# A causal dynamic convolution with layer norm and feed-forward net on one core: shorter softmax and norm steps, a first part summed by TensorE in four chunks, low halves of the weights on VectorE, and a new written order

## The chip, the cores and the metric

The kernel runs on one core of a Trainium2 chip. The metric is the device time of one launch in microseconds (us), the median of several runs; lower is better. The engines of the core are named as in the profile: PE is TensorE (matmul) and PEld its loading of weights, DVE is VectorE, ACT is ScalarE, POOL is GpSimd, SP is the engine that only issues transfers (SPq, POOLq and ACTq are the queues of issues).

## The reference

The input `x` has 8 batches of 4224 tokens of 192 features; `weight_gen` gives each token 8 heads of 7 taps. A softmax over the taps weighs a causal convolution, head by head (24 features each); a layer norm and a feed-forward net of width 768 follow, with a residual.

```python
w = weight_gen - np.max(weight_gen, axis=-1, keepdims=True)
w = np.exp(w)
w = w / (np.sum(w, axis=-1, keepdims=True) + 1e-09)
x_pad = np.concatenate([np.zeros((B, 6, D)), x], axis=1)
x_unf = x_pad[:, np.arange(S)[:, None] + np.arange(7)[None, :], :].reshape(B, S, 7, 8, 24)
x = np.einsum('bshk,bskhg->bshg', w, x_unf).reshape(B, S, D)
mu, var = mean and variance of x over its 192 features
xn = (x - mu) / np.sqrt(var + 1e-06) * g_ln
return x + np.maximum(xn @ w_ch1, 0.0) @ w_ch2      # 192 -> 768 -> 192
```

`g_ln`, `w_ch1` and `w_ch2` come as doubles.

## The kernel before

**Layout.** Each of the 128 partitions holds 264 consecutive tokens ("columns"); 16 partitions make a batch. The columns are cut three ways: into parts for the norm (six of 4, six of 8, fifteen of 12, one of 8, one of 4), into pieces for the softmax (4, 8, then 12 each), and into groups of four columns for the feed-forward net, 66 in all. A part is made of chunks of 4 or 6 columns for the convolution.

**Softmax**, piece by piece: maximum on VectorE (`max`), subtraction on GpSimd (`sub`), exponential on ScalarE (`exp`), sum on VectorE (`sum`, into an SBUF tile `sm`), an estimate of the inverse on ScalarE from logarithm and exponential (`rcp`), one Newton step on VectorE in three instructions that work in the PSUM tile `wn` (`inv`), and the product of exponentials and inverse into `wn` (`mul`).

**Convolution**, chunk by chunk. Taps 1 and 2, 3 and 4, 0, and 5 and 6 are multiplied by four instructions, `c0` to `c3`, into pair buffers `pr` (tap 0 into the output buffer `y`). Two transfers that GpSimd issues add one half of a pair to the other (`d0`, `d1`), and four additions on GpSimd sum up (`a0` to `a3`, L514). The first three chunks go another way: TensorE sums the seven products in PSUM by matmuls with an identity matrix (`z0` to `z3`, L532), ScalarE copies the sum out (L539), and the fourth product is GpSimd's, with weights that ScalarE has copied to SBUF (`keep`, L471).

**Norm and transposition.** ScalarE sums and squares each column; per part it takes the inverse root (logarithm, exponential, square: `rstd`), and VectorE refines it in five instructions (`newton`). Per group ScalarE scales (`xh`) and rounds to fp16 (`hi`, L635), GpSimd subtracts for the low half (`lo`, L648), and SP issues a transposing transfer (`turn`, L652) into `xT`. Such a transfer and GpSimd's adding transfers are kept apart by waits.

**Feed-forward net.** A group's first layer is three units of 72 half-row matmuls each, listed as x36 (L670), every unit into one of two PSUM buffers `ph`. ScalarE's relu makes the fp16 high half `hh` (L685), VectorE the low half `hlo` (L687); the `ph` buffer is free only after `hlo`. The second layer is two half outputs per group (`p0`, `p1`, L721) into the one buffer `po`, put in between the next group's units; VectorE merges `po` with the residual in `y` (`f`, L773), and SP stores. The last group's output has a form of its own (L750).

**Weights.** They are loaded as pairs of 32-bit words, turned to fp32 by bit operations on VectorE (L836 to L846), and scaled by powers of two that come from their norm (`w_scale`, L860 to L876). ScalarE makes a scaled fp16 high half and, in a second copy, a scaled fp32; GpSimd subtracts for the low half (`w_l`, L905 for the first layer, L938 for the second). For the first layer SP then swaps row halves by four transfers (`w_m`, L909), `c_w` to `c_w`. Every unit waits for all of these. Before the first unit, 11 matmuls without use for the result run on TensorE (`wake`, L642), as soon as the first high half is there.

**Order.** A table, `PLACE`, gives every operation one number; all are issued in that order, so each engine works off its own list in the order of the numbers and waits at an instruction until what it needs is there. Buffers are assigned in the same order.

## Time and profile before

| | |
|---|---|
| median of 3 runs | 869.25 us (866.22, 869.25, 870.33) |
| span of the profiled execution | 867.2 us (no other time is recorded for it) |
| TensorE busy, share of the span | 823.4 us, 95% |
| VectorE | 772.1 us, 89% |
| ScalarE | 683.7 us, 79% |
| GpSimd | 679.6 us, 78% |
| first feed-forward unit starts | 64.04 us |
| last product ends | 862.9 us |

The profile is of one execution. A busy share is a mean over the whole span: it doesn't say which engine the others wait for at a given time. Matmuls overlap in their pipeline, so rows of several matmuls give from the first start to the last end.

### The profile page before, as it was taken

The numbers are of one execution on the slowest core, as the hardware profiler recorded it, in microseconds if no ns is written. First come the engines' busy times: TensorE is split into PE (matmuls) and PEld (weight loads), VectorE is DVE, ScalarE is ACT, GpSimd is POOL, SyncE is SP. The second block draws the span as 40 slices with busy tenths as digits, with TensorE's granted clock in tenths as the row PEclk, the third lists the DMA queues.
The fourth block names the chain that finished last, engine by engine and source line by source line (L and its number), as shares of the span: only waits on it lengthen the run. The fifth ranks groups of instructions, "written<-read, shape, count | busy, mean of one in ns | idle before, by whom it ended". The sixth has DMA issues, their size and how long they took to land.

```text
span 867.2 us, 37431 instructions
## 1 busy us (share of the span) xinstructions
PE 823.4 (95%) x16665; PEld 787.7 (91%) x16665; DVE 772.1 (89%) x796; ACT 683.7 (79%) x1781; POOL 679.6 (78%) x390
## 2 busy tenths in 40 slices
...
GB/s 193 190 127 166 166 163 184 200 176 180 194 193 151 220 94 188 213 181 180 160 205 195 149 213 175 165 139 187 207 99 200 120 151 190 124 127 106 40 76 110
DMA packets 137465, 140.89 MB, mean 162 GB/s; under 512 B 107479, under 2 KB 109015, under 8 KB 137303
## 3 DMA queue, kind: packets, MB, share of 16 engines
...
q8 instruction: 130, 2.13, 1.1%
q14 instruction: 32, 0.26, 0.1%
q10 hardware_dynamic: 304, 0.00, 0.0%
...
## 4 chain that ended last, share of the span: by engine, by line
PE 68%; DVE 9%; issue 2%; DVEq 0%
PE ph L670 34%; PE po L721 34%; DVE pr L511 4%; DVE hlo L687 2%; DVE y L511 1%; DVE y L773 1%; PE ph L750 1%; DVE sm L449 0%; DVE mx L440 0%; DVE wn L465 0%; DVE wn L460 0%; DVE wn L461 0%; DVE wn L459 0%; DVE wn L599 0%; DVE wn L601 0%
## 5 line engine op out<-in xcount | busy, mean ns | idle before, releaser
L514 POOL TENSOR_TENSOR y<-y,pr 128x1152 f32<-128x1152 f32 (+1 forms) x192 | 474.5, 2499 | 39.0 <-DVE pr L511 22.1
L670 PE MATMUL ph<-xT,c_w 64*128 64x256 f16 x7128 | 420.0, 270 | 10.5 <-DVE hlo L687 7.8
L670 PEld LDWEIGHTS <-c_w 64*128 64x128 f16 x7128 | 377.6, 94 | 28.3 <-issue 13.5
L721 PE MATMUL po<-c_w2h,hh 64*128 64x192 f16 x3120 | 392.5, 243 | 1.4 <-issue 1.0
L721 PE MATMUL po<-c_w2h,hlo 64*128 64x192 f16 x3120 | 392.4, 243 | 0.5 <-issue 0.5
L721 PE MATMUL po<-c_w2l,hh 64*128 64x192 f16 x3120 | 392.4, 243 | 0.0
L721 PEld LDWEIGHTS <-hh 64*128 64x128 f16 x6240 | 345.7, 94 | 2.8 <-issue 1.9
L511 DVE TENSOR_TENSOR pr<-x,wn 128x2304 f32<-128x2304 f32 (+1 forms) x150 | 332.5, 2226 | 6.6 <-POOL y L514 1.8
L687 DVE SCALAR_TENSOR_TENSOR hlo<-ph,hh 128x1024 f16<-128x1024 f32 x198 | 239.2, 1219 | 57.2 <-ACT hh L685 56.9
L685 ACT ACTIVATE hh<-ph 128x1024 f16<-128x1024 f32 x198 | 200.3, 1015 | 105.2 <-PE ph L670 101.7
L721 PEld LDWEIGHTS <-hlo 64*128 64x128 f16 x3120 | 225.5, 94 | 0.7 <-issue 0.7
L648 POOL TENSOR_TENSOR hl<-xh,hl 128x768 f16<-128x768 f32 x66 | 115.0, 1748 | 44.5 <-ACT hl L635 33.0
L615 ACT ACTIVATE xh<-y,s 128x192 f32<-128x192 f32 x264 | 125.5, 535 | 16.1 <-DVE s L603 12.5
L569 ACT ACTIVATE junk<-y,s 128x192 f32<-128x192 f32 x264 | 119.6, 453 | 6.9
L517 POOL DMA_DIRECT2D pr<-pr x96 | 94.4, 1082 | 37.3 <-DMA xT<-hl 14.2
L564 ACT ACTIVATE junk<-y 128x192 f32<-128x192 f32 x264 | 95.1, 360 | 13.6 <-POOL y L514 7.2
L773 DVE SCALAR_TENSOR_TENSOR y<-po,c_fs,y 128x768 f32<-128x768 f32 (+1 forms) x80 | 67.9, 860 | 5.4 <-PE po L721 5.4
L511 DVE TENSOR_TENSOR y<-x,wn 128x1152 f32<-128x1152 f32 (+1 forms) x51 | 60.0, 1181 | 0.1
L635 ACT ACTIVATE hl<-xh 128x768 f16<-128x768 f32 x66 | 55.0, 837 | 2.1 <-DMA xT<-hl 1.1
L564 ACT ACTIVATION_READ_ACCUMULATOR junk<-y 128x1 f32 x264 | 49.5, 188 | 0.0
L569 ACT ACTIVATION_READ_ACCUMULATOR junk<-y,s 128x1 f32 x264 | 49.4, 187 | 0.0
L532 PE MATMUL ph<-pr,ident 128*128 128x384 f32 x72 | 27.1, 531 | 16.5 <-DVE pr L511 15.6
...
## 6 DMA issues: line engine op xcount, KB each, us to landing
...
```

The lines of the kernel that those rows point to most:

```text
L511: E.tensor_tensor(out=ov, in0=xv, in1=wv, op=ALU.mult)
L514: Q.tensor_tensor(out=flat(0), in0=flat(0), in1=flat(k), op=ALU.add)
L517: return Q.dma_start(flat(to), flat(k), accum_op=ALU.add, max_dma_last_dim=CHUNK * D * 4)
L564: A.activation(junk, at(y)[:, j, :], AF.Identity, scale=-1.0 / D, accum_out=at(s4)[:, 3, t : t + 1])
L569: A.activation(junk, at(y)[:, j, :], AF.Square, bias=at(s4)[:, 3, t : t + 1], accum_out=at(s4)[:, 0, t : t + 1])
L615: A.activation(paired(xh, t), at(y)[:, i, :].rearrange("p (c q) -> p c q", q=P // 2), AF.Identity, bias=at(s4)[:, 3, g + t : g + t + 1], s ...
L648: lambda xh=xh, hl=hl: Q.tensor_tensor(out=halves(hl, True), in0=pairs(xh), in1=halves(hl, False), op=ALU.subtract),
L670: T_.matmul(ph[:, r, v * 2 * P : (v + 1) * 2 * P], W["w1"][rows, WB[r][c], w, f : f + P], xv[rows, a, c, :, :], start=(v == 0 and k == 0), ...
L685: lambda: A.activation(at(hh)[:, us, :], at(ph), AF.Relu), [ph], [(hh, u)])
L687: lambda: V.scalar_tensor_tensor(out=at(hlo)[:, us, :], in0=at(ph), scalar=0.0, in1=at(hh)[:, us, :], op0=ALU.max, op1=ALU.subtract),
L721: made.append(T_.matmul(at(po)[:, z, e * D : (e + 1) * D], token(b, 2 * z + e, j)[rows], W[w][rows, j, :], start=(ph == 0 and e == 0 and k ...
L773: V.scalar_tensor_tensor(out=ysl, in0=at(po)[:, zs[0] : zs[-1] + 1, : 2 * D], scalar=W["fs"][:, 0:1], in1=ysl, op0=ALU.mult, op1=ALU.add)
```

## The change

- **Softmax.** The sum goes straight to PSUM, ScalarE reads it there, and the Newton step has two instructions for three. Two places in PSUM take turns.
- **Norm.** The square is written by ScalarE to PSUM with the scale in it, and `newton` has four instructions for five; two places take turns.
- **Start of the convolution.** The first part's four columns come as two chunks of two; the first four chunks (the first 12 columns, as before) are summed by TensorE, and GpSimd multiplies two of the four pairs (taps 3 and 4, and 5 and 6).
- **Weights.** The low halves are made on VectorE in one instruction that scales and subtracts; the scaled fp32 copies are gone. The second layer's scaled copy is gone as well.
- **The first half outputs** stand behind all three units of the second group, where they stood behind its second and third.
- **Order.** `PLACE` is new throughout.

```diff
 PARTS = (4,) * 6 + (8,) * 6 + (12,) * 15 + (8, 4)
-DIRECT = 3
+DIRECT = 4
+BY_POOL = (3, 5)
 PLACE = {
-    'w_l': (153, 156),
+    'w_l': (137, 166),
...
-            m = min(CHUNK, n - o) if n % CHUNK == 0 else min(4, n - o)
+            m = 2 if s0 == 0 else min(CHUNK, n - o) if n % CHUNK == 0 else min(4, n - o)
...
-        ps = WN[:, S0_ : S0_ + m]
+        ps = WN[:, S0_ + turn * MMAX : S0_ + turn * MMAX + m]
 
         step("V", v_ns(m * K), "sum",
-             lambda: V.tensor_reduce(out=at(sm)[:, :m], in_=at(e)[:, :m], axis=AX.X, op=ALU.add), [e], [sm])
+             lambda: V.tensor_reduce(out=ps, in_=at(e)[:, :m], axis=AX.X, op=ALU.add), [e], [sm])
...
-            A.activation(at(rr)[:, :m], at(sm)[:, :m], AF.Ln, bias=bias[:, 1:2])
+            A.activation(at(rr)[:, :m], ps, AF.Ln, bias=bias[:, 1:2])
...
-            V.tensor_scalar(out=ps, in0=at(sm)[:, :m], scalar1=1e-9, scalar2=None, op0=ALU.add)
-            V.tensor_tensor(out=ps, in0=ps, in1=r, op=ALU.mult)
+            V.scalar_tensor_tensor(out=ps, in0=ps, scalar=1e-9, in1=r, op0=ALU.add, op1=ALU.mult)
...
-            if direct and i == 3:
-                op("Pool", q_ns(2 * nd), (f"c{i}", t0), lambda k=k: mul(k, 2, Q), [*xr, (ch["soft"]["e"], "w")], w)
+            if direct and k in BY_POOL:
+                op("Pool", 1.89 * 2 * nd, (f"c{i}", t0), lambda k=k: mul(k, 2, Q), [*xr, (ch["soft"]["e"], "w")], w)
...
-            A.activation(row(2), row(1), AF.Square)
+            A.activation(aux(0), row(1), AF.Square, scale=D**-0.5 / A2)
...
-            V.tensor_scalar(out=aux(0), in0=row(0), scalar1=1.0 / (D * A2 * A2), scalar2=1e-6 / (A2 * A2),
-                            op0=ALU.mult, op1=ALU.add)
-            V.tensor_tensor(out=aux(1), in0=aux(0), in1=row(2), op=ALU.mult)
+            V.scalar_tensor_tensor(out=aux(1), in0=row(0), scalar=1e-6 * D, in1=aux(0), op0=ALU.add, op1=ALU.mult)
...
-        def low(dst, src, hi, n, r, w):
-            op("Pool", q_ns(n), ("w_l", 0), lambda: Q.tensor_tensor(out=dst(), in0=src(), in1=hi(), op=ALU.subtract), r, w)
+        def low(dst, src, hi, n, r, w, scale):
+            op("V", v_ns(n), ("w_l", 0),
+               lambda: V.scalar_tensor_tensor(out=dst(), in0=src(), scalar=scale, in1=hi(), op0=ALU.mult,
+                                              op1=ALU.subtract), r, w)
...
-        copy("w_h", lambda: f32(wa, F), lambda: f32(wa, F), F, ["gi"], [wa], gi[:, 0:1])
-        low(lambda: w1[:, 0, 1, :], lambda: f32(wa, F), lambda: w1[:, 0, 0, :], F, [wa, "h0"], ["l0"])
+        low(lambda: w1[:, 0, 1, :], lambda: f32(wa, F), lambda: w1[:, 0, 0, :], F, [wa, "gi", "h0"], ["l0"], gi[:, 0:1])
...
-        op("Pool", q_ns(NF * D), want2,
-           lambda: Q.tensor_tensor(out=w2g, in0=f32(w2r, NF * D), in1=w2f, op=ALU.subtract),
-           ["w2h", "fs", *wv], ["w2"])
+        op("V", v_ns(NF * D), want2,
+           lambda: V.scalar_tensor_tensor(out=w2g, in0=f32(w2r, NF * D), scalar=r2[:, 2:3], in1=w2f, op0=ALU.mult,
+                                          op1=ALU.subtract),
+           ["w2h", "r2", "fs", *wv], ["w2"])
...
+            late = prev["prev"] is not None and prev["prev"]["prev"] is None
             for u in range(3):
                 products(prev, u)
-                if u and prev["prev"]:
+                if u and prev["prev"] and not late:
                     half_output(prev["prev"], u - 1, prev["s"])
+            if late:
+                for z in range(2):
+                    half_output(prev["prev"], z, prev["s"])
```

The new order, at three places. The names are the buffers with their numbers. First GpSimd's list at the start, from its first product to the first group's low half (`hl0`); before, it read:

```order
L511 TENSOR_TENSOR pr0_76<-x_63,e0_98 128x2x768
L442 TENSOR_TENSOR e0_98<-w2_66,mx0_92 128x672
L511 TENSOR_TENSOR pr2_78<-x_63,e1_99 128x2x768
L511 TENSOR_TENSOR pr4_80<-x_63,e1_99 128x2x768
L442 TENSOR_TENSOR e0_98<-w0_64,mx1_93 128x672
L442 TENSOR_TENSOR e1_99<-w1_65,mx0_92 128x672
L517 DMA pr3_79<-pr3_79 128x768
L648 TENSOR_TENSOR hl0_83<-xh0_81,hl0_83 128x2x384
L514 TENSOR_TENSOR y3_70<-y3_70,pr0_76 128x768
L905 TENSOR_TENSOR c_w1_127<-hlo0_90,c_w1_127 128x768
```

And now (L517 is the product, L449 the softmax's subtraction, L655 the low half; the code above them is longer by some lines):

```order
L517 TENSOR_TENSOR pr3_79<-x_63,e1_97 128x2x384
L517 TENSOR_TENSOR pr0_76<-x_63,e1_97 128x2x384
L449 TENSOR_TENSOR e1_97<-w2_66,mx0_92 128x672
L517 TENSOR_TENSOR pr4_80<-x_63,e0_96 128x2x768
L517 TENSOR_TENSOR pr2_78<-x_63,e0_96 128x2x768
L517 TENSOR_TENSOR pr3_79<-x_63,e0_96 128x2x768
L517 TENSOR_TENSOR pr2_78<-x_63,e0_96 128x2x768
L449 TENSOR_TENSOR e1_97<-w0_64,mx1_93 128x672
L523 DMA pr4_80<-pr4_80 128x768
L449 TENSOR_TENSOR e0_96<-w1_65,mx0_92 128x672
L655 TENSOR_TENSOR hl0_83<-xh0_81,hl0_83 128x2x384
```

Ahead of the low half stand four wide products where two stood (a third, of the first chunk, was earlier), and four of half the width, two of them shown; the weights' low halves (L905) are gone from the list.

Second, SP's list around the first two transpositions. Before (`c_w1` is the first layer's weights; L909 swaps their row halves):

```order
L909 DMA c_w1_127<-c_w1_127 64x1536
L422 DMA w1_65<-in_weight_gen_dram 128x1x672
L909 DMA c_w1_127<-c_w1_127 64x2x384
L909 DMA c_w1_127<-c_w1_127 64x1536
L652 DMA_TRANSPOSE xT0_85<-hl0_83 128x12x128
L909 DMA c_w1_127<-c_w1_127 64x2x384
L652 DMA_TRANSPOSE xT1_86<-hl1_84 128x12x128
```

Now:

```order
L427 DMA w0_64<-in_weight_gen_dram 128x1x672
L659 DMA_TRANSPOSE xT0_85<-hl0_83 128x12x128
L918 DMA c_w1_125<-c_w1_125 64x1536 x2
L427 DMA w1_65<-in_weight_gen_dram 128x1x672
L918 DMA c_w1_125<-c_w1_125 64x2x384 x2
L659 DMA_TRANSPOSE xT1_86<-hl1_84 128x12x128
```

The first transposition stood behind three of the four swaps and now stands ahead of all.

Third, VectorE's list around the first two `hlo`. Before (L511 are products, L687 is `hlo`, L459 to L461 a softmax's Newton step):

```order
L511 TENSOR_TENSOR y6_73<-x_63,wn0_104 128x768
L511 TENSOR_TENSOR y7_74<-x_63,wn0_104 128x768
L511 TENSOR_TENSOR y8_75<-x_63,wn0_104 128x768
L687 SCALAR_TENSOR_TENSOR hlo0_90<-ph1_106,hh0_88 128x1024
L459 TENSOR_SCALAR wn0_104<-sm0_96 128x96
L460 TENSOR_TENSOR wn0_104<-wn0_104,rr0_94 128x96
L461 SCALAR_TENSOR_TENSOR wn0_104<-wn0_104,rr0_94 128x96
L687 SCALAR_TENSOR_TENSOR hlo0_90<-ph0_105,hh0_88 128x1024
```

Now (L517 and L694):

```order
L517 TENSOR_TENSOR pr1_77<-x_63,wn0_102 128x2x768
L517 TENSOR_TENSOR pr3_79<-x_63,wn0_102 128x2x768
L517 TENSOR_TENSOR pr4_80<-x_63,wn0_102 128x2x768
L870 TENSOR_SCALAR c_r2_123<-po0_105 128x1
L466 SCALAR_TENSOR_TENSOR wn0_102<-wn0_102,rr0_94 128x96
L467 SCALAR_TENSOR_TENSOR wn0_102<-wn0_102,rr0_94 128x96
L517 TENSOR_TENSOR pr2_78<-x_63,wn0_102 128x2x768
L694 SCALAR_TENSOR_TENSOR hlo0_90<-ph0_103,hh0_88 128x1024
L471 TENSOR_TENSOR wn0_102<-e1_97,wn0_102 128x672
L880 TENSOR_SCALAR c_r2_123<-c_r2_123 128x1
L882 TENSOR_SCALAR c_r2_123<-c_r2_123 128x1
L883 RECIPROCAL c_r2_123<-c_r2_123 128x1
L694 SCALAR_TENSOR_TENSOR hlo0_90<-ph1_104,hh0_88 128x1024
```

The first `hlo` stood behind three products of one tap and now stands behind four of two taps, the last of them directly ahead of it.

## Rows read from the trace of the kernel before

**Rows 1.** The first part of the page: busy time of each engine, its share of the span, and its instructions.

```profile
PE 823.4 (95%) x16665; PEld 787.7 (91%) x16665; DVE 772.1 (89%) x796; ACT 683.7 (79%) x1781; POOL 679.6 (78%) x390
```

**Rows 2.** The span cut into stretches. The columns are the stretch and its length, the busy time (and instructions) of PE, PEld, DVE, ACT and POOL, the granted share of TensorE's clock, the share in which the DMA engines are busy, and GB/s.

```profile
0.00:20.00 20.00, 6.33 (x11) 3.53 (x12) 12.84 (x25) 4.79 (x12) 7.50 (x11) 1.00 0.77 197
20.00:40.00 20.00, 17.13 (x55) 9.94 (x55) 16.96 (x28) 14.46 (x46) 5.90 (x3) 1.00 0.81 212
...
100.00:200.00 100.00, 100.00 (x2136) 100.00 (x2132) 98.57 (x112) 86.81 (x231) 94.41 (x64) 1.00 0.80 178
...
300.00:400.00 100.00, 99.98 (x2129) 99.53 (x2125) 99.10 (x92) 86.95 (x230) 91.30 (x48) 1.00 0.85 175
...
700.00:800.00 100.00, 100.00 (x2133) 99.49 (x2129) 78.60 (x78) 78.62 (x205) 81.10 (x45) 1.00 0.68 137
```

**Rows 3.** From the chain of work that ended last: start, us, engine, output and line, instructions. The first two are the pairs of units of two neighbouring groups, the third is the last group's output.

```profile
282.87 3.93 PE ph L670 x72
...
294.71 3.93 PE ph L670 x72
...
856.81 6.06 PE ph L750 x72
```

**Rows 4.** TensorE's and VectorE's instructions in order of time where the feed-forward net begins: start, us, engine, line, operation, tiles and shapes, count, and in brackets how long the engine stood idle before and what released it. x72 is two units, x36 one.

```profile
59.45 4.66 PE L642 MATMUL ph<-hl 128*128 128x512 f16 x11
64.04 4.10 PE L670 MATMUL ph<-xT,c_w 64*128 64x256 f16 x72
...
72.08 1.22 DVE L687 SCALAR_TENSOR_TENSOR hlo<-ph,hh 128x1024 f16<-128x1024 f32 x1
...
73.35 6.08 PE L670 MATMUL ph<-xT,c_w 64*128 64x256 f16 x72 [5.21 <-DVE hlo L687]
...
81.60 0.22 PEld L721 LDWEIGHTS <-hh 64*128 64x128 f16 x4
```

**Rows 5.** The same view of VectorE, ScalarE, GpSimd and SP's queue between 10 and 60 us.

```profile
11.77 1.75 DVE L511 TENSOR_TENSOR pr<-x,wn 128x1536 f32<-128x1536 f32 x1 [1.80 <-DMA x<-in_x_dram]
...
25.82 0.80 ACT L539 COPY y<-ph 128x768 f32<-128x768 f32 x1 [5.07 <-PE ph L532]
...
36.06 2.91 POOL L511 TENSOR_TENSOR pr<-x,e 128x1536 f32<-128x1536 f32 x1 [6.03 <-ACT pr L849]
...
42.90 0.83 ACT L635 ACTIVATE hl<-xh 128x768 f16<-128x768 f32 x1
...
44.79 1.94 POOL L648 TENSOR_TENSOR hl<-xh,hl 128x768 f16<-128x768 f32 x1
...
53.09 1.19 POOL L905 TENSOR_TENSOR c_w<-hlo,c_w 128x384 f16<-128x384 f32 x1
...
56.39 1.60 SPq L652 DMA_TRANSPOSE xT<-hl  x1
...
58.05 0.64 SPq L909 DMA_DIRECT2D c_w<-c_w  x1
```

**Rows 6.** Transfers issued in the first 90 us: what, the queue, how many, KB each, median us from issue to landing.

```profile
x<-in_x_dram SPq DMA_DIRECT2D x1, 900.0 KB, 7.8
...
c_w<-c_w SPq DMA_DIRECT2D x2, 96.0 KB, 3.9
```

**Rows 7.** Instructions grouped by line and shape over the whole span, of VectorE and then of GpSimd: line, engine, operation, tiles, shapes, count | busy us, mean ns of one | idle before.

```profile
L511 DVE TENSOR_TENSOR pr<-x,wn 128x2304 f32<-128x2304 f32 x90 | 228.4, 2545 | 0.6 <-POOL y L514 0.3
L511 DVE TENSOR_TENSOR pr<-x,wn 128x1536 f32<-128x1536 f32 x60 | 104.1, 1746 | 6.0 <-DMA x<-in_x_dram 1.8 <-POOL y L514 1.6 <-PE po L860 1.4
...
L511 DVE TENSOR_TENSOR y<-x,wn 128x1152 f32<-128x1152 f32 x30 | 40.4, 1345 | 0.1
...
L459 DVE TENSOR_SCALAR wn<-sm 128x96 f32<-128x96 f32 x21 | 5.3, 254 | 0.2
...
L597 DVE TENSOR_SCALAR wn<-s 128x12 f32<-128x12 f32 x15 | 2.5, 169 | 0.8 <-ACT junk L569 0.2
...
L846 DVE SCALAR_TENSOR_TENSOR hlo<-pr,po 128x384 f32<-128x384 f32 x3 | 1.6, 544 | 0.0
...
L846 DVE SCALAR_TENSOR_TENSOR hlo<-pr,ph 128x768 f32<-128x768 f32 x1 | 0.9, 947 | 0.0
...
L514 POOL TENSOR_TENSOR y<-y,pr 128x768 f32<-128x768 f32 x72 | 143.8, 2045 | 10.6 <-DVE y L511 4.8 <-DVE pr L511 2.5 <-DMA pr<-pr 1.8
...
L511 POOL TENSOR_TENSOR pr<-x,e 128x1536 f32<-128x1536 f32 x3 | 8.7, 2904 | 17.5 <-ACT e L471 7.2 <-ACT pr L849 6.0 <-DMA x<-in_x_dram 4.3
L938 POOL TENSOR_TENSOR c_w2l<-hlo,c_w2h 128x1152 f16<-128x1152 f32 x1 | 3.0, 3002 | 0.0
L905 POOL TENSOR_TENSOR c_w<-hlo,c_w 128x768 f16<-128x768 f32 x1 | 1.6, 1642 | 0.0
```

**Rows 8.** VectorE's and TensorE's instructions in order of time around 174 us, columns as in rows 4: the 27th `hlo`, and the two units beside it.

```profile
173.44 1.22 DVE L687 SCALAR_TENSOR_TENSOR hlo<-ph,hh 128x1024 f16<-128x1024 f32 x1
...
173.66 4.11 PE L670 MATMUL ph<-xT,c_w 64*128 64x256 f16 x72
```

**Rows 9.** What TensorE waited for between 95 and 790 us: us in total, how many times, the longest.

```profile
PE ph L670 <- issue: 2.5, 2, 1.4
PE ph L670 <- DVE hlo L687: 2.3, 5, 1.0
PE po L721 <- issue: 1.5, 2, 1.0
```

More of the change, by code (lines that the diff above doesn't have):

```diff
@@ new lines @@
+    'w_load': (23, 1, 6, 25, 3, 5),
+    'w_load2': (52,),
+    'w_as': (77,),
+    'w_av': (78, 79, 80, 86),
+    'w_an': (91,),
+    'w_cs': (44,),
+    'w_cv': (24, 36, 37, 45),
+    'w_cn': (46,),
+    'w_s1': (111, 115, 122, 127, 132),
+    'w_h': (133, 148),
+    'w_l': (137, 166),
+    'w_m': (149, 147, 170, 172),
+    'w_c2s': (96, 140, 174),
+    'w_c2v': (84, 90, 93, 97, 130, 135, 139, 145, 157, 163, 167, 178),
+    'w_c2n': (100, 150, 179),
+    'w_s2': (189, 196, 205, 213, 215, 217, 228),
@@ new lines @@
+    'max': (12, 8, 43, 63, 101, 171, 218, 424, 314, 496, 694, 584, 939, 1108, 930, 1111, 1263, 1261, 1498,
+        1560, 1644, 1739, 1923),
+    'sub': (14, 10, 57, 114, 124, 229, 334, 435, 564, 666, 773, 874, 959, 1153, 1078, 1257, 1386, 1449,
+        1588, 1690, 1796, 1876, 1967),
+    'exp': (16, 15, 64, 123, 156, 264, 371, 473, 577, 674, 786, 929, 1025, 1173, 1109, 1270, 1448, 1455,
+        1597, 1697, 1817, 1892, 1976),
+    'sum': (21, 17, 67, 126, 160, 325, 388, 485, 601, 718, 812, 947, 1027, 1186, 1137, 1271, 1454, 1485,
+        1602, 1781, 1863, 1990, 1992),
@@ new lines @@
+    'squares': (88, 81, 128, 116, 162, 169, 186, 193, 253, 260, 269, 288, 312, 305, 355, 357, 385, 418, 426,
[7 rows of a table added]
+    'rstd': (89, 129, 175, 206, 268, 301, 358, 430, 505, 576, 649, 735, 822, 919, 1026, 1120, 1234, 1325,
+        1414, 1530, 1617, 1720, 1831, 1929, 2024, 2121, 2226, 2301, 2348),
+    'newton': (95, 134, 180, 223, 279, 322, 364, 443, 511, 590, 655, 748, 825, 921, 1030, 1122, 1237, 1328,
[13 rows of a table added]
+    'wake': (138,),
[4 rows of a table added]
+    'turn': (146, 176, 237, 247, 329, 374, 407, 417, 475, 467, 556, 546, 636, 625, 689, 681, 775, 785, 851,
[21 rows of a table added]
@@ L199 @@
+    'halo': (245, 645, 891, 1138, 1378, 1780, 2076),
+    'unit': (187, 195, 219, 221, 235, 236, 261, 276, 289, 304, 315, 333, 345, 360, 372, 394, 395, 415, 428,
[11 rows of a table added]
+    'relu': (204, 202, 220, 231, 244, 256, 273, 278, 297, 318, 321, 346, 366, 363, 381, 397, 409, 421, 440,
[11 rows of a table added]
+    'hlo': (214, 208, 232, 234, 262, 257, 283, 299, 307, 331, 342, 352, 369, 367, 384, 406, 410, 425, 447,
[15 rows of a table added]
+    'hop': (248, 290, 338, 386, 414, 445, 487, 518, 566, 609, 641, 679, 712, 747, 788, 807, 855, 889, 918,
[17 rows of a table added]
 }
@@ L326 @@
     S0_ = MMAX * K
-    X0_ = S0_ + MMAX
+    X0_ = S0_ + 2 * MMAX
+    assert X0_ + 6 * PMAX <= 2 * HALF
     def at(b):
```

88 lines of the change are left out of this document (28 added, 60 removed), and 240 rows, old and new, of the table PLACE.

## The prediction

> **What bounds the kernel now.** I read the busy shares first, then the slices by stretch, then TensorE's own row of instructions, and last the lists of VectorE and GpSimd around the place where TensorE's stream begins. TensorE is busy 823.4 us of 867.2 [rows 1], and from 100 us on it is busy without a break [rows 2]: a group of four columns takes 294.71 - 282.87 = 11.84 us there [rows 3], and 66 groups are 781.4 us. The last product ends at 856.81 + 6.06 = 862.87 [rows 3]; what follows to 867.2 is 4.3 us of merge and store. The first feed-forward product starts at 64.04 [rows 4]. So the span is 64.0 (start) + 781.4 + 4.3 + 17.4 us in which the stream stood still. Of these 17.4, one stretch lies at the start: by 81.60, where the first half output begins, five units are done [rows 4]; five units are 5 x 1.97 = 9.8 us of the 17.56 since 64.04, so 7.7 is lost. The other 9.7 is scattered over 780 us.
>
> The second thing to see is VectorE: 98.6 us of the 100 from 100 on and 99.1 of the 100 from 300 on, and only 78.6 from 700 to 800 [rows 2]. For the first half of the run it has as little room as TensorE; later it has much. An instruction saved on VectorE late in the run is worth nothing; one saved before the stream starts, or while VectorE is full, may be.
>
> So the time can change in three ways: the stream starts earlier, it stands still for less at the start, or VectorE and GpSimd (94.4 and 91.3 us of 100 in the same stretches) fail to follow a stream that is earlier. TensorE's own work is the same: 198 units, 130 half outputs, the last four outputs; the first part is split, but its columns are gathered either way.
>
> **What is removed and added, on VectorE.** All durations are rows 7. Each softmax loses one step of three: 23 x 0.25 = 5.8 us. Each norm loses one of five: 29 x 0.17 = 4.9 us. The products of taps 3 and 4 of the first 12 columns go to GpSimd: 3 x 1.75 = 5.2 us. Three low halves come from GpSimd: 0.95 + 0.55 + 1.34, 2.8 us if they cost as the other steps of these widths. Net -13 us, of which the 10.7 in small steps is spread over the run; after 400 us VectorE's own idle time hides it. The reductions now write PSUM and ScalarE reads it; the old first step already read one memory and wrote the other at 254 ns, so I put the move at nothing, bounds -0.1 and +0.1 us each; 23 of them make 2 us at most, late ones hidden.
>
> GpSimd gains 3 x 2.90 = 8.7 us of products and loses 1.64 + 1.19 + 3.00 = 5.8 (two rows of low halves, the third estimated from the row at 53.09 [rows 5]). ScalarE loses three copies of the weights, some 2.8 us; it is busy 79% [rows 1] and on the path only where it evicts the first units.
>
> **The start, step by step.** Before, the first unit hangs on two chains [rows 5]. One is part 0: gathered and copied at 25.82, high half at 42.90, low half 44.79 to 46.7, and then the transposition is issued only at 56.39, because on SP it stands behind three of the weights' swaps (the second fence of rows of the order). The third waits for GpSimd's second low half (53.09), and the fourth swap is issued last, at 58.05; its row lands in 3.9 us [rows 6]. The wake-up products from 59.45 end at 64.1.
>
> After, the transposition stands ahead of all swaps on SP, and the low halves stand on VectorE. I walk down the lists with the row durations. The first x load is 720 KB for 900 KB, so the first product starts about 0.8 us before 11.77 [rows 5, 6]. Columns 0 to 3 come as two small chunks; the second is gathered and copied by 24, against 25.82. GpSimd then runs four wide products in a row, 4 x 2.9, with one stop: the third needs a buffer that ScalarE holds for the weights until about 30.5. It ends near 36, where before its third product began (36.06). High half near 37, low half on GpSimd near 40 to 42, transposition near 44. The weights: VectorE's second low half stands 70 instructions into its list, near 50.5 to 51; the swaps are issued at 51 and 51.7 and land 3.9 later: the first unit starts near 55.6, 8.4 earlier.
>
> The eviction that frees the third unit is a second, independent reading. Before, VectorE's list up to and with its first `hlo` has 106 instructions whose rows sum to 68.1 us; it ends at 72.08 + 1.22 = 73.30 [rows 4], 5.2 later (it stands idle for 10.2 us in the first 40 alone [rows 2]; neighbours overlap a little). After, that list has 87 instructions and 57.4 us: 7.8 less of products, 2.7 of softmax steps, 1.4 of norm steps, 1.5 more of weights. With 5.2 again it ends at 62.6; ScalarE's list, which must evict first, reaches that point near 63.3 in the walk, so I take 63.9. The third unit then starts at 64.0 for 73.35. The fourth `hlo` stands 8.8 us of rows later, at 72.7; the sixth unit starts at 73.5 and the first half output at 75.4. Taking off the sixth unit, which the new order puts ahead of it, this is 73.5 against 81.60: the stream is 8.1 ahead.
>
> Two charges. The first two units run after a pause of some 8 us behind the wake-up products; before, a pause of 5.2 us was followed by units at the lower clock (6.08 for 3.93 [rows 4]). That costs up to 1.9 per unit, but both wait for the eviction at 63.3 anyway: nothing, at most 1.9. And the low halves read both operands from SBUF on VectorE while GpSimd adds; no row of before shows such a pair. Bounds: nothing, and one add of 2.05 [rows 7] for each of the two ahead of the first unit, 4.1. I take 1. The stream is 7.1 ahead.
>
> **Does it stay ahead?** VectorE is full, so `hlo` can't come earlier than its list lets it. Before, the 27th `hlo` ends at 174.66, and the unit that needs its buffer starts at 175.6, 1.0 later [rows 8]. After, the list up to the 27th `hlo` is 168.0 for 173.1: 5.1 shorter. So about there the stream can be 5.1 + 1.0 = 6.1 ahead, no more. The other places are looser (8 us shorter at the 50th, 8.4 at the 100th, 12.7 at the end). Past the tight place TensorE is the bound again, and part of the 2.3 us that it waited for `hlo` between 95 and 790 [rows 9] goes, some 1. The 4.0 of "issue" waits stays. Gain: 6.1 + 1 = 7.1, less 0.5 for GpSimd, whose list before the low half of the 22nd group is 4.6 longer. 6.6 off 867.2 is 860.6, and 862.5 as a median if the profiled span stands to the runs as before (867.2 to 869.25).
>
> **Rivals.**
> - *The lead is given back (866.5).* If GpSimd's four products and the buffer that ScalarE holds push parts 3 to 5 back, VectorE and GpSimd are both full and the lead shrinks to what they allow. For it: rows 2. Against it: VectorE's list is shorter everywhere. Gain 2 to 3.
> - *VectorE and GpSimd block each other (865.5).* Each of the three low halves waits out a GpSimd instruction, 2.0 us, and holds the next one; the path to the first half output passes all three, so 3 x 1.2 on average comes off the gain. The Trainium skill, "SBUF — State Buffer", section "Who interferes with whom", says that a VectorE instruction with two SBUF inputs contends with a GpSimd one that reads SBUF; by that rule this rival is the likelier one for these three instructions. No run yet shows it here.
> - *Slower (876).* In the new order `hlo` often stands one or two products later. A pair of 1.75 (2.5 in wide chunks) ahead of it makes TensorE wait when the 1.0 us of rows 8 is all the room there is. 0.2 us a group is 13 us, and 862.5 + 13 is 875.5. It turns to a loss from 0.1 us a group on. For it: the third fence of rows of the order. Against it: the place where VectorE was tightest comes out 6.1 ahead with the new positions counted in.
> - *More (857).* If the tight place isn't tight (VectorE's idle time before 60 us falls as well), the 8.1 stays and the later waits go too: 11 to 12.
>
> **Numbers.** Forecast 0.50, given back 0.14, blocking 0.13, slower 0.13, more 0.10. This kernel tells 0.5% (4.3 us) from no change: faster is under 864.9, slower above 873.6. Faster: nearly all of the forecast and of "more", a third of blocking, together 0.63. Slower: most of the last but one, 0.11. Same: 0.26. The range leaves out the slow rival and a little of the gains: 856.5 to 869. The likeliest case alone spans 859 to 866 (the 4.1 of blocking, the 1.9 of the clock, and 2 us of gain not counted).
>
> **What the new profile would show.** Right: the first unit near 55 to 57, the first half output near 75 to 77 behind six units, group period 11.84 from 100 us on, VectorE still near 99% to 300 us and idler later than now. Wrong: a first unit past 60 (then the weights' chain or the swaps' landing is misjudged); TensorE waiting for `hlo` by more than 3 us in total between 95 and 400 (then the order took the lead back); low halves on VectorE much longer than 0.95, 0.55 and 1.34 (blocking).

## The result and the profile after

The changed kernel takes 880.88 us (median of 4 runs, 878.94 to 882.65). The kernel before took 869.1 us in the runs beside it. The ratio is 1.0143, with a 95% interval of 1.0117 to 1.0169: the change makes the kernel slower, by 12 us, where 862.5 was forecast. The range, 856.5 to 869, does not hold it. The profiled execution has a span of 878.5 us.

The first part of its page, which answers to [rows 1]:

```profile
PE 826.2 (94%) x16693; PEld 800.4 (91%) x16693; DVE 768.4 (87%) x747; ACT 681.0 (78%) x1779; POOL 683.9 (78%) x392
```

VectorE has 49 instructions fewer, but it is busy only 3.7 us less, where 13 were forecast. By stretches, columns as in [rows 2]:

```profile
100.00:200.00 100.00, 95.27 (x2016) 93.88 (x2012) 97.00 (x105) 82.28 (x215) 90.08 (x60) 1.00 0.77 167
...
700.00:800.00 100.00, 100.00 (x2126) 99.94 (x2123) 82.94 (x78) 77.78 (x194) 73.43 (x40) 1.00 0.59 123
```

TensorE was busy for all of the 100 us from 100 on and is now for 95.27. VectorE, GpSimd and ScalarE are each less busy there too, so none of them is fuller: they wait for one another. In the last stretch TensorE is as busy as before. What TensorE waits for between 95 and 790 us, columns as in [rows 9]:

```profile
PE ph L677 <- DVE hlo L694: 12.7, 12, 2.2
PE po L728 <- DVE y L780: 3.0, 3, 1.5
```

The wait for `hlo` was 2.3 us in total and is 12.7. The start, TensorE alone, columns as in [rows 4]:

```profile
54.98 3.59 PE L677 MATMUL ph<-xT,c_w 64*128 64x256 f16 x31 [5.48 <-DMA c_w<-c_w]
58.51 1.44 PE L867 MATMUL po<-c_s,ones 128*128 128x1 f32 x6
59.88 4.02 PE L677 MATMUL ph<-xT,c_w 64*128 64x256 f16 x36
66.27 2.14 PE L677 MATMUL ph<-xT,c_w 64*128 64x256 f16 x36 [2.38 <-DVE hlo L694]
69.35 2.14 PE L677 MATMUL ph<-xT,c_w 64*128 64x256 f16 x36 [0.94 <-DVE hlo L694]
75.26 5.45 PE L677 MATMUL ph<-xT,c_w 64*128 64x256 f16 x72 [3.77 <-DVE hlo L694]
80.53 0.26 PE L728 MATMUL po<-c_w2h,hh 64*128 64x192 f16 x2
```

The first unit comes where it was forecast (55.6; five of its matmuls run before). The third comes at 66.27 for the forecast 64.0, and the first half output at 80.53 for 75.4.

**What `hlo` waits for.** The waits of ScalarE and VectorE between 80 and 800 us show three lines that the kernel before has not at all, and one (the third) that has grown: engine, output and line, what released it, total us, count, longest.

```profile
ACT rr L459 <- DVE pr L517: 13.0, 9, 3.2
...
ACT wn L603 <- DVE pr L517: 6.3, 6, 1.5
DVE wn L606 <- ACT wn L603: 5.3, 8, 2.4
...
DVE pr L517 <- ACT wn L603: 4.4, 3, 1.9
```

The third is the norm's step waiting for its own square. The kernel before has it too:

```profile
DVE wn L599 <- ACT s L594: 2.0, 4, 0.7
```

L459 is the softmax's logarithm, L603 the norm's square. Neither uses a product (L517). But the logarithm now reads its sum in `wn`, and the square is written into `wn`: the PSUM tile from which VectorE's products read their weights. In the built program 14 of the 23 logarithms and 24 of the 29 squares wait for a product of VectorE; before the change none did. One such place, VectorE's instructions and then ScalarE's:

```profile
400.90 0.85 DVE L456 TENSOR_REDUCE wn<-e 128x96 f32<-128x672 f32 x1
401.86 2.55 DVE L517 TENSOR_TENSOR pr<-x,wn 128x2304 f32<-128x2304 f32 x1
405.23 2.55 DVE L517 TENSOR_TENSOR pr<-x,wn 128x2304 f32<-128x2304 f32 x1 [0.82 <-POOL y L520]
409.42 2.35 DVE L694 SCALAR_TENSOR_TENSOR hlo<-ph,hh 128x1024 f16<-128x1024 f32 x2 [1.63 <-ACT hh L692]
```

```profile
403.67 1.00 ACT L692 ACTIVATE hh<-ph 128x1024 f16<-128x1024 f32 x1
407.82 0.34 ACT L459 ACTIVATE rr<-wn,bias 128x96 f32<-128x96 f32 x1 [3.15 <-DVE pr L517]
408.19 0.28 ACT L460 ACTIVATE rr<-rr 128x96 f32<-128x96 f32 x1
408.38 1.00 ACT L692 ACTIVATE hh<-ph 128x1024 f16<-128x1024 f32 x1
```

The sum is ready at 401.75. ScalarE comes to the logarithm at 404.67 and stands 3.15 us, until the second product has ended at 407.78. Behind it the relu (L692) stands; `hlo` waits 1.63 for it; and the next row of the chain that ended last is TensorE's:

```profile
409.42 1.24 DVE hlo L694
410.70 4.11 PE ph L677 x72
```

So the reading is that ScalarE and VectorE take turns on a tile, and that ScalarE's other work queues up behind its turn. The Trainium skill, "PSUM — Partial Sum Buffer", section "PSUM bank collisions raise a hardware error", says that two engines must not use one bank (in the same quarter of the partitions) at once, reads included, and that software guards by bank, not by address. The waits above are in the program, and they guard more than the columns that are touched: of the 38 products waited for, 13 read columns 0 to 511 of `wn` alone, while sum and square lie from column 672 on. So the guard is by the whole tile, which is two halves of 512 columns. No run here left a wait out, or narrowed one.

### The profile page after: what moved, and what is told of

Same layout as the page of the kernel before. It is cut to its first block, busy times and chain, and to the rows that moved or that the text cites. A ratio compares the mean times of both kernels' runs of the same rounds, so it can differ in the third digit from the quotient of the medians.

```text
span 878.5 us, 37400 instructions
## 1 busy us (share of the span) xinstructions
PE 826.2 (94%) x16693; PEld 800.4 (91%) x16693; DVE 768.4 (87%) x747; ACT 681.0 (78%) x1779; POOL 683.9 (78%) x392
## 4 chain that ended last, share of the span: by engine, by line
PE 33%; POOL 13%; DMA 7%; DVE 7%; ACT 4%; issue 4%; SPq 0%; POOLq 0%; DVEq 0%; ACTq 0%
PE ph L677 17%; PE po L728 16%; POOL y L520 9%; DMA xT<-hl 4%; DVE pr L517 4%; DMA pr<-pr 3%; POOL hl L655 2%; DVE hlo L694 2%; ACT hh L692 2%; POOL pr L523 1%; ACT junk L575 1%; PE ph L757 1%; DVE y L780 1%; ACT xh L622 0%; ACT hl L642 0%
## 5 line engine op out<-in xcount | busy, mean ns | idle before, releaser
L677 PEld LDWEIGHTS <-c_w 64*128 64x128 f16 x7128 | 382.2, 95 | 46.1 <-issue 24.6
L728 PE MATMUL po<-c_w2h,hh 64*128 64x192 f16 x3120 | 388.3, 243 | 4.3 <-DVE y L780 3.0
L728 PE MATMUL po<-c_w2l,hh 64*128 64x192 f16 x3120 | 388.3, 243 | 0.0
L728 PE MATMUL po<-c_w2h,hlo 64*128 64x192 f16 x3120 | 388.2, 243 | 0.0
L517 DVE TENSOR_TENSOR pr<-x,wn 128x2304 f32<-128x2304 f32 (+2 forms) x148 | 327.7, 2223 | 13.2 <-ACT wn L603 4.4
L728 PEld LDWEIGHTS <-hh 64*128 64x128 f16 x6240 | 312.9, 94 | 6.4 <-issue 3.8
L694 DVE SCALAR_TENSOR_TENSOR hlo<-ph,hh 128x1024 f16<-128x1024 f32 x198 | 239.5, 1219 | 62.5 <-ACT hh L692 61.9
L692 ACT ACTIVATE hh<-ph 128x1024 f16<-128x1024 f32 x198 | 199.3, 1013 | 109.8 <-PE ph L677 108.0
L728 PEld LDWEIGHTS <-hlo 64*128 64x128 f16 x3120 | 184.4, 94 | 0.0
L655 POOL TENSOR_TENSOR hl<-xh,hl 128x768 f16<-128x768 f32 x66 | 114.5, 1743 | 43.1 <-ACT hl L642 30.3
L523 POOL DMA_DIRECT2D pr<-pr x96 | 92.4, 1014 | 65.4 <-DMA xT<-hl 34.1
L517 DVE TENSOR_TENSOR y<-x,wn 128x1152 f32<-128x1152 f32 (+2 forms) x52 | 60.3, 1162 | 2.1 <-ACT rr L459 0.8
L449 POOL TENSOR_TENSOR e<-w,mx 128x672 f32<-128x672 f32 (+2 forms) x23 | 33.4, 1453 | 7.1 <-DVE wn L471 4.0
```

The lines of the kernel that those rows point to most:

```text
L517: E.tensor_tensor(out=ov, in0=xv, in1=wv, op=ALU.mult)
L523: return Q.dma_start(flat(to), flat(k), accum_op=ALU.add, max_dma_last_dim=CHUNK * D * 4)
L655: lambda xh=xh, hl=hl: Q.tensor_tensor(out=halves(hl, True), in0=pairs(xh), in1=halves(hl, False), op=ALU.subtract),
L677: T_.matmul(ph[:, r, v * 2 * P : (v + 1) * 2 * P], W["w1"][rows, WB[r][c], w, f : f + P], xv[rows, a, c, :, :], start=(v == 0 and k == 0), ...
L692: lambda: A.activation(at(hh)[:, us, :], at(ph), AF.Relu), [ph], [(hh, u)])
L694: lambda: V.scalar_tensor_tensor(out=at(hlo)[:, us, :], in0=at(ph), scalar=0.0, in1=at(hh)[:, us, :], op0=ALU.max, op1=ALU.subtract),
```

## The experiments

Three theories stood against each other: turns on the shared tile; VectorE and GpSimd blocking each other where a VectorE instruction reads two operands from SBUF (the low halves of the weights); and the new order by itself.

### Sum and square out of the shared tile

With the short steps kept, and only the place of sum and square changed (e1), or of the sum alone (e2):

```diff
-V.tensor_reduce(out=ps, ...)
+V.tensor_reduce(out=SM[:, turn, :m], ...)
-V.scalar_tensor_tensor(out=ps, in0=ps, scalar=1e-9, in1=r, ...)
+V.scalar_tensor_tensor(out=ps, in0=SM[:, turn, :m], scalar=1e-9, in1=r, ...)
# e1 alone:
-A.activation(aux(0), row(1), AF.Square, scale=D**-0.5 / A2)
+A.activation(row(2), row(1), AF.Square, scale=D**-0.5 / A2)
```

> The changed kernel with the softmax sum and the norm's square written to SBUF again, all else as changed. Theory A (shared tile: ScalarE's logarithm and square wait for whatever product of VectorE stands ahead of them, because sum and square lie in the tile that the products read): the 13.0 us in which ScalarE's L459 and the 4.4 in which its L603 waited for products go, and of TensorE's 22.6 us of stalls between 80 and 870 us some 13 go: 866 to 870 us. Rival B (the new order itself: hlo stands behind products, GpSimd's adding transfers behind transpositions, wherever the sums lie): 878 to 881 us.

> The changed kernel with only the softmax sum back in SBUF; the norm's square stays in PSUM. Theory A: the larger part of the two, three quarters of the waits (13.0 of 17.4 us): 869 to 874 us. Rival B: 878 to 881 us.

Measured: e1 921.52 us, ratio 1.0617 (1.0572 to 1.0661); e2 892.77, 1.0245 (1.0178 to 1.0313). Both are far slower than the changed kernel and than either theory expected. In e1 the waits of logarithm and square for a product are gone, in e2 the logarithm's, and something dearer has come. VectorE's first Newton steps in e1 (L467 softmax, L607 norm), grouped by shape:

```profile
L467 DVE SCALAR_TENSOR_TENSOR wn<-sm,rr 128x96 f32<-128x96 f32 x21 | 22.3, 1062 | 0.4 <-ACT rr L461 0.2
L607 DVE SCALAR_TENSOR_TENSOR wn<-s 128x12 f32<-128x12 f32 x15 | 20.9, 1396 | 4.5 <-ACT s L604 3.9
...
L609 DVE SCALAR_TENSOR_TENSOR wn<-wn,s 128x12 f32<-128x12 f32 x15 | 2.7, 178 | 0.5
```

The step with both operands in SBUF takes 1396 ns, the step of the same shape with one operand in PSUM 178. With the tiles as they lie here, the short form has either two operands in SBUF (and this price) or one in PSUM (and the turns). The three-step form before, one operand at a time from SBUF into PSUM, pays neither. A place in PSUM away from the tile that the products read was not tried.

### The short steps alone, in the order of before

```diff
 # e5, on the kernel before; e4 the same with sum and square in PSUM, three places for the sum
-V.tensor_scalar(out=ps, in0=sm, scalar1=1e-9, scalar2=None, op0=ALU.add)
-V.tensor_tensor(out=ps, in0=ps, in1=r, op=ALU.mult)
+V.scalar_tensor_tensor(out=ps, in0=sm, scalar=1e-9, in1=r, op0=ALU.add, op1=ALU.mult)
```

> The kernel before, with its own order, given only the shorter softmax and norm steps, sum and square in PSUM. Theory A: ScalarE waits for products here too (the list has 11 logarithms and 15 squares that would wait for one): slower than the same steps in SBUF by 4 to 14 us, 870 to 880 us. Rival B: as the same steps in SBUF, 865 to 869 us.

> The kernel before, with its own order, given only the shorter softmax and norm steps, sum and square left in SBUF: 10.7 us fewer of small steps on VectorE. Both theories: 865 to 869 us, since TensorE sets the pace from 100 us on and the order is not moved; below 865 would say that VectorE's steps were on the path.

Measured: e4 964.72, 1.1115 (1.1085 to 1.1145); e5 913.16, 1.052 (1.0479 to 1.0562). Both theories had expected far less. In e4, VectorE's and TensorE's waits (80 and 100 to 800 us; ScalarE's square is L598, its logarithm L454):

```profile
DVE wn L461 <- ACT wn L598: 19.3, 2, 11.2
...
DVE pr L512 <- ACT wn L598: 16.0, 5, 5.7
...
DVE pr L512 <- ACT rr L454: 8.8, 3, 3.8
```

```profile
PE ph L672 <- DVE hlo L689: 41.7, 21, 7.9
```

VectorE stands up to 11.2 us until ScalarE has had its turn. In an order not made for the turns they cost near 100 us (e4 less e16, below); the new order makes most of them short. Not all of the 100 is waiting. The busy times of e4, and then of e16, which has the same TensorE instructions:

```profile
PE 844.9 (88%) x16665; PEld 814.9 (85%) x16665; DVE 765.6 (79%) x744; ACT 683.6 (71%) x1781; POOL 679.2 (71%) x390
```

```profile
PE 821.8 (95%) x16665; PEld 791.9 (92%) x16665; DVE 762.7 (88%) x744; ACT 684.3 (79%) x1781; POOL 679.0 (79%) x390
```

TensorE is busy 23 us longer for the same work, because part of it ran at the 1.2 GHz level behind longer pauses. The granted clock from 700 to 800 us is 0.90 in e4 and 1.00 in e16, and the two units that start at 727.79 in e4, behind a pause of 7.92 us, took 6.69 us where such a pair took 4.11 at 706.98. In e5 the wide step takes 1660 ns, where the step before on one operand takes 254 [rows 7]:

```profile
L459 DVE SCALAR_TENSOR_TENSOR wn<-sm,rr 128x96 f32<-128x96 f32 x21 | 34.9, 1660 | 0.2
L596 DVE SCALAR_TENSOR_TENSOR wn<-s 128x12 f32<-128x12 f32 x15 | 26.5, 1767 | 3.4 <-ACT s L593 2.9
```

Two operands in SBUF aren't slow by themselves. Three of these steps in order of time:

```profile
339.98 7.23 DVE L459 SCALAR_TENSOR_TENSOR wn<-sm,rr 128x96 f32<-128x96 f32 x1
...
698.53 0.18 DVE L596 SCALAR_TENSOR_TENSOR wn<-s 128x12 f32<-128x12 f32 x1 [0.59 <-ACT s L593]
...
700.59 0.26 DVE L459 SCALAR_TENSOR_TENSOR wn<-sm,rr 128x96 f32<-128x96 f32 x1
```

The last two ran while GpSimd stood idle (698.45 to 703.89). Of the 52 steps in e5, 9 ran with no GpSimd instruction beside them and took 0.17 to 0.26 us. All 31 that took over 0.4 us ended 0.03 to 0.14 us behind the end of a GpSimd instruction; the first of the three lay across four of them.

### The long steps in the new order

e6 is the changed kernel with the softmax's three steps and the norm's five as before; e10 takes back the norm alone, e11 the softmax alone.

```diff
-V.scalar_tensor_tensor(out=ps, in0=ps, scalar=1e-9, in1=r, op0=ALU.add, op1=ALU.mult)
+V.tensor_scalar(out=ps, in0=SM[:, turn, :m], scalar1=1e-9, scalar2=None, op0=ALU.add)
+V.tensor_tensor(out=ps, in0=ps, in1=r, op=ALU.mult)
-A.activation(aux(0), row(1), AF.Square, scale=D**-0.5 / A2)
-V.scalar_tensor_tensor(out=aux(1), in0=row(0), scalar=1e-6 * D, in1=aux(0), ...)
+A.activation(row(2), row(1), AF.Square)
+V.tensor_scalar(out=aux(0), in0=row(0), scalar1=1.0 / (D * A2 * A2), ...)
+V.tensor_tensor(out=aux(1), in0=aux(0), in1=row(2), op=ALU.mult)
```

> The changed kernel, new order and new start, with the longer steps of before: the softmax sum in SBUF and three Newton instructions, the norm's square in SBUF and five. VectorE has 10.7 us more of small steps, but none of them has both operands in SBUF, and ScalarE's logarithm and square have no wait for a product. Theory A (with sum and square in the products' PSUM tile, ScalarE and VectorE take turns on it; the waits hold relu and hlo): TensorE's stalls between 80 and 870 us fall from 22.6 us to 12 or less and the time to 866 to 872 us. Rival B (the order alone does it): 880 to 886 us.

> The changed kernel with the norm's five steps of before and its square in SBUF; the softmax keeps its sum in PSUM and its two steps. It takes away ScalarE's 6.3 us of waits at L603 and VectorE's 10.5 us of waits for L603 between 80 and 800 us, and adds 4.9 us of small steps. Theory A: most of the gain of the run with all old steps (9.1 us): 873 to 877 us if the norm is the larger part; 878 to 881 if the softmax is.

> The changed kernel with the softmax's three steps of before and its sum in SBUF; the norm keeps its square in PSUM and its four steps. It takes away ScalarE's 13.0 us of waits for products at L459 and adds 5.8 us of small steps. Theory A: 872 to 876 us if the softmax is the larger part, 877 to 881 if the norm is. The two runs' gains add up to about 9 if they are independent.

Measured: e6 871.8, 1.0038 (1.0021 to 1.0055); e10 878.26, 1.0106 (1.0065 to 1.0146); e11 874.63, 1.006 (1.0043 to 1.0077). Against 880.88 the softmax's steps give back 6.2 and both 9.1. The norm's give 2.6, which is not clear of the noise (e10 875.73 to 882.52, the changed kernel 878.94 to 882.65); so that the two add up fits, but isn't shown by the times. All three lie in a range of the theory of turns. The waits go with them one by one. ScalarE in e10, and then in e11:

```profile
ACT rr L459 <- DVE pr L517: 13.7, 9, 3.9
```

```profile
ACT wn L605 <- DVE pr L519: 6.9, 6, 1.8
```

Each kernel keeps one of the two waits, as large as in the changed kernel, and has lost the other. So the turns are the greater part of the loss. But e6, without any of them, is still 3.1 us behind its kernel before (868.73 in that set).

### The low halves and the start

e7 puts the first layer's low halves back on GpSimd, with ScalarE's scaled copies; e8 puts the first two relus and `hlo`s in the order of their units; e9 is e6, e7 and e8 together. e12 is e6 with the second layer's low half back on GpSimd. e13 is e6 with all low halves there, the second right behind the first, the swaps issued early, and the relus in the order of their units.

```diff
 # e7, e13 (e12 in the same way for the second layer)
-op("V", ..., lambda: V.scalar_tensor_tensor(out=dst(), in0=src(), scalar=scale, in1=hi(), ...), r, w)
+op("Pool", q_ns(n), ("w_l", 0), lambda: Q.tensor_tensor(out=dst(), in0=src(), in1=hi(), op=ALU.subtract), r, w)
 # e8, e13
-'relu': (204, 202, 220, ...     'hlo': (214, 208, 232, ...
+'relu': (202, 204, 220, ...     'hlo': (208, 214, 232, ...
 # e13
-'w_l': (137, 166), 'w_m': (149, 147, 170, 172)
+'w_l': (137, 137.5), 'w_m': (149, 147, 149.5, 149.6)
```

> The changed kernel with the first layer's two low halves made by GpSimd from scaled copies of ScalarE, as before, at the places that they have now. If VectorE's 2.04 and 2.16 us for them (0.95 and 0.55 by width) are waiting for GpSimd's operand port, they go and VectorE reaches its first hlo 3 to 4 us earlier: the first half output 2 to 4 us earlier, the time 876 to 879 us; 880 to 882 us if the later waits set the end whatever the start.

> The changed kernel with the first group's first two relu, and its first two hlo, in the order of their units (the new order has the second unit's ahead, so that ScalarE waits 1.6 us for it). If that wait is on the path: third unit 1.6 to 2.5 us earlier than 66.3, and the time 878 to 880 us; if VectorE's list of the next microseconds sets it, the same as the changed kernel, 880 to 882 us.

> The three edits together: steps of before, the first layer's low halves on GpSimd, relu in the order of the units. Theory A: the start is ahead of the kernel before by 5 us or more and the later stalls are like those of before: 861 to 867 us. Rival B: 876 to 883 us.

> All old steps in the new order, as the run of 871.8 us, and the second layer's low half on GpSimd, as before, at its new place. On VectorE that one instruction took 2.7 us in the changed kernel, 3.6 and 9.7 us in two of the runs, for 1.34 us by width, just ahead of the third and fourth hlo. If it waits for GpSimd's operand port on the path to the fourth unit: the first half output 1 to 3 us earlier and the time 868 to 871 us; if GpSimd's list then holds the next low halves back by its 3.0 us: 871 to 874 us.

> All old steps in the new order, all three low halves on GpSimd, the first layer's second one right behind the first, its swaps issued right behind, and relu in the order of the units: no instruction of VectorE with two SBUF operands is left. If the start can be kept: first unit near 51 us, first hlo near 61, first half output 5 to 8 us ahead of the kernel before, and the time 862 to 868 us. If VectorE's list between 100 and 300 us sets the stream whatever the start: 868 to 872 us, with the stream level with that of the kernel of before by the 20th group.

Measured: e7 883.98, 1.0186 (1.0158 to 1.0214); e8 883.29, 1.0175 (1.0138 to 1.0211); e9 878.68, 1.0109 (1.0058 to 1.0159); e12 871.97, 1.0039 (1.0021 to 1.0057); e13 871.37, 1.0028 (1.001 to 1.0047). None gains anything against the kernel that it edits (880.88 for e7 and e8, 871.8 for the others), and e9 loses. e7 and e8 lie above both of their expected ranges, the others in the slower of their two.

The blocking itself is there. The low halves on VectorE in the changed kernel took more than twice what they would by width (1.34, 0.55 and 0.95 us):

```profile
L945 DVE SCALAR_TENSOR_TENSOR c_w2l<-hlo,c_r,c_w2h 128x1152 f16<-128x1152 f32 x1 | 2.7, 2698 | 0.0
...
L913 DVE SCALAR_TENSOR_TENSOR c_w<-hlo,c_gi,c_w 128x384 f16<-128x384 f32 x1 | 2.2, 2157 | 0.0
L913 DVE SCALAR_TENSOR_TENSOR c_w<-hlo,c_gi,c_w 128x768 f16<-128x768 f32 x1 | 2.0, 2039 | 0.0
```

And in e9, where GpSimd happened to have work without a gap, the widest took 9.71 us, with `hlo` behind it. VectorE, and then GpSimd:

```profile
71.43 9.71 DVE L948 SCALAR_TENSOR_TENSOR c_w2l<-hlo,c_r,c_w2h 128x1152 f16<-128x1152 f32 x1
81.06 2.34 DVE L698 SCALAR_TENSOR_TENSOR hlo<-ph,hh 128x1024 f16<-128x1024 f32 x2
```

```profile
71.43 1.63 POOL L450 TENSOR_TENSOR e<-w,mx 128x672 f32<-128x672 f32 x1
72.75 2.07 POOL L522 TENSOR_TENSOR y<-y,pr 128x768 f32<-128x768 f32 x1
74.51 1.90 POOL L659 TENSOR_TENSOR hl<-xh,hl 128x768 f16<-128x768 f32 x1
76.11 3.80 POOL L522 TENSOR_TENSOR y<-y,pr 128x768 f32<-128x768 f32 x2
```

The instruction begins with GpSimd's run of five (the last row is two) and ends 1.2 us after it, at 81.14. In this trace group 2, counted as below, starts at 94.05, 8.6 us behind e6, and the lag is still there at group 20 (318.58 for 309.95); that is e9's loss here. Its four runs span 871.23 to 881.45 us and the traced one is the slowest, so the instruction may have been held for less in the others, which weren't traced. It doesn't explain the end time of the others, since a lead at the start isn't kept. When the first unit of a group starts, groups counted from 0, from each trace:

| group | before | after | e6 | e13 |
|---|---|---|---|---|
| 2 | 89.61 | 86.75 | 85.46 | 83.54 |
| 6 | 138.15 | 138.77 | 135.85 | 135.55 |
| 8 | 161.82 | 162.44 | 159.58 | 159.28 |
| 20 | 306.36 | 312.15 | 309.95 | 309.96 |
| 65 | 844.82 | 856.19 | 846.67 | 847.46 |

e13 leads by 6.1 us at group 2 and by 2.5 at group 8, where it has met e6. At group 20 both are 3.6 behind the kernel before. A start 2 us better is worth nothing 75 us later.

### Short steps without either price

To price the steps alone, the first step of each Newton step is replaced by one of the same shape that reads one operand in SBUF and writes the constant 1 to PSUM; the correction is then left out of the result. VectorE has as many instructions as in the changed kernel. e14 is that in the new order, e15 that with e13's start, e16 that in the order of before.

```diff
-V.scalar_tensor_tensor(out=ps, in0=ps, scalar=1e-9, in1=r, op0=ALU.add, op1=ALU.mult)
+V.tensor_scalar(out=ps, in0=SM[:, turn, :m], scalar1=0.0, scalar2=1.0, op0=ALU.mult, op1=ALU.add)
-V.scalar_tensor_tensor(out=aux(1), in0=row(0), scalar=1e-6 * D, in1=aux(0), ...)
+V.tensor_scalar(out=aux(1), in0=row(0), scalar1=0.0, scalar2=1.0, op0=ALU.mult, op1=ALU.add)
```

> The changed kernel with as many small steps as it has (two per softmax, four per norm) but none that conflicts: the first step of each reads one SBUF operand only and the sum and the square lie in SBUF. It leaves the Newton correction out (the first step writes the constant 1), so its output is the estimate of ScalarE alone. If turns on the PSUM tile are the whole price of the shorter steps, it is faster than the run with the longer steps (871.8 us) by part of the 10.7 us that VectorE no longer spends: 865 to 870 us. If VectorE's small steps are off the path in the new order: 870 to 873 us.

> The same conflict-free short steps (the Newton correction left out) with the start of the run of 871.4 us: low halves on GpSimd, the first layer's swaps early, relu in the order of the units. If it is VectorE's list between the second and the twentieth group that gave the early start back, the stream stays ahead longer here: 860 to 867 us. If it is the order of the other engines (GpSimd's adding transfers behind the transpositions, ScalarE's relu behind its sums): 868 to 872 us.

> The kernel before, its own order, with the same conflict-free short steps (the Newton correction left out): 10.7 us less on VectorE and nothing else. If VectorE's small steps are on the path there, 861 to 866 us; if the order hands the time to other waits, 866 to 870 us.

Measured: e14 868.24, 0.9995 (0.9977 to 1.0014); e15 867.29, 0.9986 (0.9969 to 1.0004); e16 864.93, 0.9957 (0.9944 to 0.9969), beside a kernel before of 868.81. e14 lies in the range that has the turns as the whole price of the short steps, e16 in the one that has VectorE's small steps on the path, and e15 between its two. e16 is e5 with another first step: the row of 1660 ns above is 254 here.

```profile
L459 DVE TENSOR_SCALAR wn<-sm 128x96 f32<-128x96 f32 x21 | 5.3, 254 | 0.2
```

The steps are 52 in all (23 and 29). e5 less e16 is 48.2 us, or 0.93 us for each step with two operands in SBUF; e1 less e14, in the other order, is 53.3. (TensorE is busy 11.3 us longer in e5, 833.1 for 821.8, so not all of the 48.2 need be waiting.) The Trainium skill, "SBUF — State Buffer", section "Who interferes with whom", has VectorE's second pair of SBUF ports shared with GpSimd, under a lock that only one holds. The rows agree: 1660 ns with two operands against 254 with one, and 0.26 us with two while GpSimd stands idle.

The turns are then after less e14, 12.6 us. e14 also leaves out the norm's wait for its own square; by runs with whole results it is after less e6, 9.1, and the 3.9 of the steps (e16), 13.0.

The new order by itself, with its start, is e14 less e16, 3.3 us, as in e6 (3.1). In the traces e14 is 1.4 ahead at group 8 (159.26 against 160.69) and 2.2 behind at group 65 (842.90 against 840.75), so it loses 3.6 in between. One such place, GpSimd in e15, which was 5.9 ahead of e16 at group 2 and is 0.9 behind at group 20:

```profile
292.95 0.88 POOL L524 DMA_DIRECT2D pr<-pr  x1 [5.34 <-DMA xT<-hl]
```

An adding transfer of GpSimd is kept apart from a transposition and waits 5.34 us for it. Whether such places make up all of the 3.6 us was not tried by itself and stays open.

## Why the prediction was wrong

From before to after, in us, with what each step rests on:

| step | us | from |
|---|---|---|
| before | 868.8 | |
| shorter steps, no price, order of before | -3.9 | e16 |
| new order and start, low halves on VectorE | +3.3 | e14 less e16 |
| turns on the shared tile | +12.6 | after less e14 |
| after | 880.9 | |

- **The step that failed** is "I put the move at nothing, bounds -0.1 and +0.1 us each; 23 of them make 2 us at most". The durations did stay near: 856 ns for a sum and 335 for a logarithm, for 844 and 363 before. Two rows of before, and two of after:

```profile
L449 DVE TENSOR_REDUCE sm<-e 128x96 f32<-128x672 f32 x21 | 17.7, 844 | 0.0
```

```profile
L452 ACT ACTIVATE rr<-sm,bias 128x96 f32<-128x96 f32 x21 | 7.6, 363 | 1.1 <-DVE sm L449 1.1
```

```profile
L456 DVE TENSOR_REDUCE wn<-e 128x96 f32<-128x672 f32 x21 | 18.0, 856 | 1.3 <-ACT wn L603 0.8
```

```profile
L459 ACT ACTIVATE rr<-wn,bias 128x96 f32<-128x96 f32 x21 | 7.0, 335 | 14.8 <-DVE pr L517 13.0 <-DVE wn L456 0.9 <-DVE wn L471 0.8
```

  The idle time behind the bar is what the bounds left out: 14.8 us before 21 logarithms, 13.0 of it for products. At the end of the run the turns of both, sum and square, cost 12.6 us (after less e14). I costed the move by how long an instruction takes, and not by who else holds the tile. The square, moved too, I did not cost at all. That VectorE was busy 98.6 of 100 us [rows 2] should have told me that whoever must wait for its product finds no gap.
- **The saved steps** were worth 3.9 us at the end (e16), for 10.7 that the forecast took off VectorE's list (its busy time fell by 9.4). That they count was right in kind. That "after 400 us VectorE's own idle time hides it" was read from too few stretches: before, VectorE is busy 97.88 of the 100 us from 500 on, and e16's lead over the kernel before still grows from 2.5 us at group 20 to 4.0 at group 40.
- **The tight place.** The 27th `hlo` ends at 176.1 for 174.66 before. VectorE's rows up to there sum to 171.6 us for 172.6 before (neighbours overlap a little), so 1.0 less where 5.1 was forecast. The low halves are the rest: 2.04 + 2.16 + 2.70 for 2.84 is 4.1. The charge of 1 us for them was too small, by 3 us of VectorE. But taking them off gains nothing: in e13 VectorE's rows up to there sum to 167.8 and it is idle for 17.0 (14.3 before), and its 27th `hlo` ends at 173.5, 1.2 earlier than before for rows that are 4.8 shorter. A shorter list is not an earlier `hlo`: the list's own waits grow when it runs ahead.
- **The start.** The first unit was right (54.98 for 55.6), in part by luck: the last swaps were issued at 52.03 for 51, and landed in 2.2 us for 3.9. The third was 2.3 late. Of this, 1.1 is VectorE idle ahead of its first `hlo`: the new order has the second unit's relu ahead of the first's, and that unit took 4.02 us at a granted clock of 0.5, the 1.2 GHz level (the third number from the end of the row below, columns as in [rows 2]). "But both wait for the eviction at 63.3 anyway: nothing, at most 1.9" missed that the eviction itself waits for the slow unit. In e8, which mends the order and where that unit took 2.14 us, VectorE doesn't wait there and the third unit still starts at 65.42: the rest is VectorE's list, which comes later than forecast. It decided nothing: e8 ends no earlier.

```profile
60.00:64.00 4.00, 3.90 (x36) 2.53 (x34) 3.71 (x5) 2.29 (x9) 3.15 (x3) 0.50 0.95 225
```

- **The rivals.** "The lead is given back" happened, as the table of groups shows; whether for the reason that the rival gives was not tried. "Block each other" was right in mechanism, and its 1.2 us each is near the 4.1 that the three took too long, but that is not where the time went. "Slower (876)" had the sign and was close in size, but its reason, `hlo` behind products, has room only in what the order loses, 3.3 us at the end; the other 12.6 are mostly `hlo` behind a relu behind a logarithm or square behind a product. The sign of being wrong, more than 3 us of waits for `hlo` between 95 and 400, came true with 6.7, but "the order took the lead back" is the smaller part of the cause.
